# Routing attention and an MLP mixer: queries of the first pairs by rows of 1536 bytes, ahead of the keys, and an earlier turn of the second pair's queries

## Chip, cores and metric

The kernel runs on one core of a Trainium2 chip. The metric is the device time of one execution in microseconds (us): the median of three runs, and beside it one execution taken with the hardware profiler, from which all rows of the profile come. The core's engines are PE (TensorE, matmuls; PEld are its weight loads), DVE (VectorE), ACT (ScalarE), POOL (GpSimd) and SP (SyncE, which issues most transfers). Sixteen DMA engines carry the transfers.

## What is computed

Attention with a cluster mask for 4 batches of 8 heads, 768 tokens and 64 dimensions, then a mixer over tokens and over channels:

```python
q_assign = argmax(einsum('bhsd,hcd->bhsc', q_n, c_n), -1)   # c_n: 16 normed centroids a head
k_assign = argmax(einsum('bhsd,hcd->bhsc', k_n, c_n), -1)
mask = q_assign[:, :, :, None] == k_assign[:, :, None, :]
scores = where(mask, q @ k.T / 8, -1e9)
x = softmax(scores) @ v                                      # to (4, 768, 512)
u = x + (relu(x.T @ w_tok1) @ w_tok2).T                      # tokens: 768 -> 256 -> 768
out = u + relu(u @ w_ch1) @ w_ch2                            # channels: 512 -> 1536 -> 512
```

All is float32, and q, k, v, the centroids and the weights lie in HBM. The centroids must be normed; queries and keys need not be for the argmax.

## The kernel before

One tile, `arena`, holds everything in SBUF; `Buf` gives a view of it by offset. One PSUM tile `ps` has 8 banks. So the profile names nearly all operands `arena` and `ps`, and operations are told apart by line and shape.

**Order.** Nothing is issued directly. Every operation is recorded in a `Program` with the engines it may run on and a cost, what it reads and what it writes (`g.add`; `mm`, `turn`, `copy`, `tt`, `vec` and `dma` are wrappers, lines 844 to 906). `Program.run` plans: PE keeps the order of the recording; the other engines take, among the operations that are ready by the planned times, the one with the earliest due time. The plan gives one fixed order for each engine's queue and decides which of two allowed engines takes an operation. On the chip each queue runs in that order, and semaphores, which are set for overlapping ranges of a tile, hold an instruction back until its inputs are there. A change in a cost, in a transfer's planned time (`more`, `early`, `after`) or in the recording can therefore move instructions elsewhere.

**Stages.** 32 heads are worked in 16 pairs `m` of two heads. For a pair, keys and queries are laid as T: [128 = 2 heads x 64, 12 blocks of 128 tokens], six blocks of keys, then six of queries. `route(m)` multiplies T by the block matrix `cbd` of normed centroids (four matmuls of 32 columns, line 846), and DVE finds each token's cluster (lines 1098 to 1103: transpose from PSUM, maximum by group, comparison, transpose back). The result becomes, in bf16, a matrix M of 0 and a large number, which adds the mask to the scores as a second matmul. `scores(m)` does 12 chunks: first the plain scores (`plain`), then the mask matmul, then an exponential on ACT (line 1205). `values` multiplies by v (line 1238). Then come the token mixer (from about 325 us) and the channel mixer, both with seven products in place of eight, whose sums run on DVE and POOL.

**The start.** For pairs 3 and up, T is made with transfers (`part_qk`, `join_qk`). For the first three it is made on PE: `load_qk` brings keys and queries of a pair with four transfers of 192 KB, one for each head of each, to `qks`: 128 partitions, 6 tokens a partition, the two heads side by side, so in pieces of 256 bytes. `turn_qk` turns 12 blocks of [128 tokens, 2 x 64] with PE into three banks, and three copies of 128 x 512 bring them to T. `begin` (line 946) issues in this order: centroids on SP; k and q of pair 0, one head of each on SP and one on ACT; k and q of pair 1. While transfers run, `keep_busy(12)` multiplies the identity by itself on PE. `norm` (lines 980 to 998) is one operation on DVE, with a square root on ACT in its middle (line 984): it norms the centroids as soon as they have landed. They are turned on PE into bank 7 and copied to `cbd` with two DVE copies (line 867). `route(0, 3)` follows. Its masks go to `M0` in eight small placements (lines 1124 to 1136), each of which ACT or DVE may do. In `scores(0)` the first three chunks of plain scores and then the turns of pair 1 stand ahead of the first mask matmul; `route(1)` follows the third:

```python
        ahead = 3 if m == 0 else 0
        for n in range(ahead):
            plain(n)
        if m == 0:
            turn_qk(1, (7, 6, 7))
            load_qkr(3, 18.0)
```

Pair 2 is turned amid `values` of pair 0.

Of the kernel before, what the change touches and what calls it, by code (L numbers as in the profile page):

```python
# [15 lines left out]
ACT = mybir.ActivationFunctionType  # L16
# [31 lines left out]
W = 64  # L48
SUM_LO, SUM_HI = 1e-15, 1e15
GRAIN = 32  # L50
BUSY, HITS_AT = 12, 18.0
CHECK_AT = 532.0
FOLD = "-VVVVVVVVVV-----"

# [669 lines left out]
def kernel(  # L724
# [43 lines left out]
    def buf(kb, shape, dt=F32):  # L768
        return Buf(arena, int(kb * 256), shape, dt)
# [13 lines left out]
    rcps = [Buf(arena, 384 + 32 * i, [2, 2, NJ]) for i in range(2)]  # L783
    dall = Buf(arena, 448, [NP, 2, NJ])

    qks = [buf(3 + 6 * i, [2, NJ, 2, D]) for i in range(2)]
    vs = [buf(15 + 3 * i, [2, NJ, D]) for i in range(3)]
    Ts = [buf(24 + 6 * i, [NQK, P]) for i in range(3)]
    Ms = [buf(42 + 3 * i, [2, S], BF16) for i in range(2)]
# [50 lines left out]
    def bank(*i):  # L840
        return [("ps", n) for n in i]
# [56 lines left out]
    def vec(fn, c, rd, wr, early=0.0, after=0.0):  # L898
        return g.add({"DVE": c - 0.08}, lambda e: fn(), rd, wr, after=after, early=early)

    def dma(dst, src, rd, wr, kb, row, after=0.0, queue="SP"):

        q = {"SP": nc.sync, "ACT": nc.scalar, "POOL": nc.gpsimd}[queue]
        return g.add(
            {queue: ISSUE}, lambda e: q.dma_start(dst, src), rd, wr, (kb * 1024, row), after  # L905
        )

    def transpose(dst, src, rd, wr, kb):
# [3 lines left out]
        )  # L912


    def load_qk(m, after=0.0, queues=("SP", "SP")):
        b, hp = divmod(m, H // 2)
        t = qks[m % 2]
        for i, a in ((1, k), (0, q)):
            for h, qu in enumerate(queues):
                dma(  # L920
                    t.ap[:, i, :, h],
                    a[b, 2 * hp + h].rearrange("(p j) d -> p j d", p=P),
                    [], [("qk", m % 2, i, h)] + (t.rows(i, i + 1) if h else []), 192, 256,
                    after, qu,
                )

    def load_qkr(m, after=0.0):
        b, hp = divmod(m, H // 2)
# [16 lines left out]

    def begin():
        cen, sq = rt[0], rt[1]
        dma(cen.ap[:, 0:D], centroids.rearrange("h c d -> (h c) d"), [], cen.k(), 32, 256)
        load_qk(0, 0.0, ("SP", "ACT"))
        load_qk(1, 1.0)  # L950
        load_v(0, 9.0)
        load_v(1, 26.0)
        g.add({"POOL": 1.0}, lambda e: make_identity(nc, ident.ap), [], ident.k())
        def consts():
            nc.vector.memset(ones.ap, 1.0)
            nc.vector.memset(msc.ap[0 : P // 2, 0:1], 1.0)
# [12 lines left out]

        vec(consts, 0.8, [], ones.k() + msc.k() + cbd.k() + want.k() + unsc.k() + low.k())  # L970
        vec(lambda: nc.vector.memset(M0.ap, 0.0), 0.5, [], M0.k())
        keep_busy(BUSY)

        def col(i):
            return nsq.ap[:, i : i + 1]

        def norm(e):
            c = cen.ap[:, 0:D]
            ss, lo, nrm, rr, tw = (col(i) for i in range(5))
            nc.vector.tensor_tensor(out=sq.ap[:, 0:D], in0=c, in1=c, op=ALU.mult)  # L980
            nc.vector.reduce_sum(out=ss, in_=sq.ap[:, 0:D], axis=AX.X)

            nc.vector.tensor_scalar_max(out=lo, in0=ss, scalar1=float(2.0**-100))
            nc.scalar.sqrt(nrm, lo)

            for it in range(2):
                nc.vector.reciprocal(out=rr, in_=nrm)
                nc.vector.scalar_tensor_tensor(
                    out=tw, in0=ss, scalar=rr, in1=nrm, op0=ALU.mult, op1=ALU.add
                )  # L990
                nc.vector.tensor_scalar(
                    out=nrm, in0=tw, scalar1=0.5, scalar2=(1e-6 if it else 0.0),
                    op0=ALU.mult, op1=ALU.add,
                )
            nc.vector.reciprocal(out=rr, in_=nrm)
            for i in range(2):
                nc.vector.tensor_scalar_mul(
                    out=sq.ap[:, i * D : (i + 1) * D], in0=c, scalar1=rr
                )

        g.add({"DVE": 4.0}, norm, cen.k(), sq.k() + nsq.k())
        turn_qk(0, (0, 1, 2), (0, 1))
        turn(ps[:, 7, 0:P], sq.ap[:, 0:P], sq.k(), bank(7))
        turn_qk(0, (0, 1, 2), (2,))
        g.add(
            {"ACT": 1.5},
            lambda e: nc.scalar.activation(out=col(5), in_=col(1), func=ACT.Exp, scale=0.0),
            nsq.k() + Ts[0].k(), [("table",)],
        )
        for i in range(2):  # L1010
            copy(
                cbd.ap[i * D : (i + 1) * D, :, i * C : (i + 1) * C],
                ps[i * D : (i + 1) * D, 7, 0:P].rearrange("p (a i c) -> p a i c", i=2, c=C)[:, :, i],
                64, bank(7), cbd.k(), ("DVE",),
            )


        def own():
            nc.vector.tensor_reduce(
                out=heads.ap, in_=ident.ap.rearrange("p (a h c) -> p h a c", h=2, c=C),  # L1020
                axis=AX.XY, op=ALU.add,
            )
            for i in range(2):
                nc.vector.tensor_scalar(
                    out=msc0.ap[:, i], in0=heads.ap, scalar1=(BIG, -BIG)[i], scalar2=None,
                    op0=ALU.mult,
                )

        vec(own, 0.7, ident.k() + nsq.k(), heads.k() + msc0.k())

    def keep_busy(n):

        for _ in range(n):
            mm(ps[:, 5, 0:P], ident.ap, ident.ap, True, True, 0.22, ident.k(), bank(5))

    def turn_qk(m, banks, parts=range(3)):
        src, T = qks[m % 2], Ts[m % 3]
        for n in parts:
            bk = banks[n]
            for i in range(4):  # L1040
                a, j = divmod(4 * n + i, NJ)
                a = 1 - a
                turn(
                    ps[:, bk, i * P : (i + 1) * P],
                    src.ap[:, a, j].rearrange("p h d -> p (h d)"),
                    [("qk", m % 2, a, 0), ("qk", m % 2, a, 1)] + src.rows(a, a + 1), bank(bk),
                )

            copy(
                T.ap[:, 4 * n : 4 * n + 4].rearrange("p a t -> p (a t)"), ps[:, bk], 512,  # L1050
                bank(bk), T.rows(4 * n, 4 * n + 4),
            )

    def part_qk(m):
# [24 lines left out]
    def route(m, bk):  # L1079
# [4 lines left out]
        for gr in range(4):  # L1084
            r0 = (NJ + HJ * gr) % NQK
            mm(
                ps[32 * gr : 32 * gr + 32, bk, 0:HS], cbd.ap[:, hp],
                T.ap[:, r0 : r0 + HJ].rearrange("p a t -> p (a t)"), True, True, 0.161,
                T.rows(r0, r0 + HJ) + cbd.k(), bank(bk), pos=(0, 32 * gr),
            )  # L1090
        a, e, o = rt[0:3]
        if m == 0:
# [68 lines left out]
    def scores(m):  # L1161
# [8 lines left out]
        def plain(n):  # L1170
            u, i = chunk(n)
            s, r0 = n % 3, NJ + HJ * u
            for h in range(2):
                hs = slice(64 * h, 64 * h + 64)
                mm(
                    ps[:, 2 * s + h, 0:HS], T.ap[hs, i],
                    T.ap[hs, r0 : r0 + HJ].rearrange("p a t -> p (a t)"), True, False, 0.3225,
                    T.rows(i, i + 1) + T.rows(r0, r0 + HJ), bank(2 * s + h), pos=(64 * h, 0),
                )

        ahead = 3 if m == 0 else 0
        for n in range(ahead):
            plain(n)
        if m == 0:
            turn_qk(1, (7, 6, 7))
            load_qkr(3, 18.0)
        for n in range(2 * NJ):
            u, i = chunk(n)
# [139 lines left out]
    def pair(m):  # L1328
# [4 lines left out]
            next_qk(m)  # L1333
        for i in range(NJ):
            if i == 3 and m == 0:
                turn_qk(2, (1, 2, 3))
            if i == 4 and 1 <= m < NP - 2:
                route(m + 2, 0)
            if i == 1:
                if m:  # L1340
                    sums(m - 1, 5)
                    finish_x(m - 1, 5, 1)
                add_up(m)
            values(m, i)
# [624 lines left out]

    begin()  # L1970
    load_qk(2, 9.0)
    route(0, 3)
    token_weights()
    channel_weights(1, 12.0)
    channel_weights(2, 180.0)
# [80 lines left out]
```

## Time and profile before

| | us |
|---|---|
| median of three runs | 789.86 (789.45 to 791.11) |
| the profiled execution | 789.87 |
| its span, first to last instruction | 788.0 |
| PE busy | 777.8 |
| DVE busy | 675.2 |
| ACT busy | 461.4 |
| POOL busy | 194.1 |

Rows of the profile give times from the start of the span. A group row reads: line, engine, operation, out<-in by tile names, shapes, count | busy us, mean ns of one | idle time just before and what ended it. A row of a stretch of time gives the busy time of each engine in it, then the granted clock of PE (1.00 is full), the DMA engines' mean busy share and GB/s. Matmuls overlap in the pipeline, so a busy PE is not PE at its peak.

### The profile page before, as it was taken

Reading aid. Unit: us, or ns where it says so; the run is one execution under the profiler, and the core shown is the slowest. Engines: PE = TensorE matmul, PEld = TensorE weight load, DVE = VectorE, ACT = ScalarE, POOL = GpSimd, SP = SyncE. Lnnn points to the kernel's source line nnn. Section 1 sums busy time; section 2 is a strip of 40 time slices with the busy share of each in tenths; the row PEclk is TensorE's granted clock in tenths of the full one; section 3 lists DMA queues with packets and bytes.
Section 4 is the critical chain, followed back from the end, with each engine's and each line's share of the span. In section 5 each row is a group of like instructions: output and inputs, shape, how many; then the busy total and the mean of one; then the engine's idle time right before and its main releaser. Section 6 shows DMA issues by size and latency. Waiting matters only on the chain.

```text
span 788.0 us, 15324 instructions
## 1 busy us (share of the span) xinstructions
PE 777.8 (99%) x5975; PEld 463.1 (59%) x5975; DVE 675.2 (86%) x848; ACT 461.4 (59%) x614; POOL 194.1 (25%) x187
## 2 busy tenths in 40 slices
PE   8999999999999999999999999999999999999996
PEld 5666666666666666545555555555555555555554
DVE  6979999999998999999999877999853576799964
ACT  5788888889889875599614368633235204400422
POOL 0000000000000000001274598700285289830000
PEclk9999999999999999999999999999999999999999
DMA  9676668876778953568848999975788744444666
GB/s 249 169 192 180 170 154 221 212 202 178 196 196 215 266 178 128 127 135 202 195 124 253 313 281 266 273 189 132 168 189 177 165 100 101 105 105 102 160 164 161
DMA packets 326576, 143.68 MB, mean 182 GB/s; under 512 B 260192, under 2 KB 322400, under 8 KB 326496
## 3 DMA queue, kind: packets, MB, share of 16 engines
q1 hardware_dynamic: 324128, 141.83, 71.6%
q8 instruction: 49, 0.80, 0.4%
q10 hardware_dynamic: 2368, 0.79, 0.4%
q14 instruction: 31, 0.25, 0.1%
HBM read 91.95 MB, written 28.61 MB: 153 GB/s over the span
## 4 chain that ended last, share of the span: by engine, by line
PE 95%; DVE 3%; DMA 1%; issue 0%; ACT 0%; SPq 0%
PE ps L846 77%; PE ps L1238 18%; DVE arena L885 2%; DMA arena<-in_q_dram 1%; DMA arena<-in_moe_w_ch_dram 0%; ACT arena L865 0%; DVE arena L1384 0%; DVE arena L1390 0%; DVE arena L1387 0%; SPq L905 0%; DVE arena L1380 0%; DVE arena L867 0%; ACT arena L1129 0%
## 5 line engine op out<-in xcount | busy, mean ns | idle before, releaser
L846 PE MATMUL ps<-arena 128*128 128x384 f32 (+5 forms) x2727 | 640.2, 463 | 4.5 <-POOL arena masks.py:199 1.4
L846 PEld LDWEIGHTS ps<-arena 128*128 128x128 f32 (+2 forms) x2343 | 340.1, 184 | 250.3 <-issue 61.6
L885 DVE TENSOR_TENSOR arena<-arena 128x1536 f32<-128x1536 f32 (+6 forms) x340 | 369.9, 1109 | 12.5 <-issue 3.6
L885 POOL TENSOR_TENSOR arena<-arena 128x384 f32<-128x384 f32 x181 | 193.4, 1109 | 501.8 <-DVE arena L885 378.6
L885 DVE TENSOR_TENSOR arena<-ps,arena 128x384 f32<-128x384 f32 (+3 forms) x227 | 189.4, 844 | 78.4 <-PE ps L846 76.0
L875 ACT COPY arena<-arena 128x768 uint16<-128x768 uint16 x221 | 189.2, 955 | 62.6 <-DMA arena<-arena 32.8
L1205 ACT ACTIVATE arena<-ps 128x768 f32<-128x768 f32 x192 | 150.7, 811 | 35.2 <-PE ps L846 33.4
L1238 PE MATMUL ps<-arena 128*32 128x192 f32 (+1 forms) x3248 | 144.9, 335 | 0.0
L1238 PEld LDWEIGHTS ps<-arena 128*32 128x32 f32 x3248 | 103.7, 110 | 44.1 <-issue 15.6
L865 ACT COPY arena<-ps 128x512 f32<-128x512 f32 (+2 forms) x44 | 31.3, 719 | 116.1 <-PE ps L846 114.8
L892 ACT ACTIVATE arena<-arena 128x1152 f32<-128x1152 f32 (+1 forms) x38 | 39.7, 1070 | 51.0 <-DVE arena L885 50.3
L1912 ACT ACTIVATE arena<-arena 128x768 f32<-128x768 f32 x40 | 38.7, 969 | 32.8 <-DMA arena<-in_moe_w_ch_dram 27.1
L846 PEld LDWEIGHTS <-arena 64*128 64x128 bf16 x384 | 19.2, 94 | 24.6 <-issue 0.2
L1390 DVE SCALAR_TENSOR_TENSOR arena<-arena 128x512 f32<-128x512 uint32 (+1 forms) x31 | 21.5, 713 | 0.4
L1384 DVE SCALAR_TENSOR_TENSOR arena<-arena 128x512 uint32<-128x512 uint32 (+1 forms) x31 | 20.9, 695 | 0.3
L1108 ACT ACTIVATE arena<-arena 128x384 bf16<-128x384 f32 x16 | 11.2, 701 | 13.6 <-issue 13.6
L1380 DVE TENSOR_SCALAR arena<-arena 128x512 uint32<-128x512 uint32 (+1 forms) x31 | 13.9, 458 | 4.0 <-DMA arena<-in_moe_w_tok_dram 4.0
L1285 DVE STREAM_TRANSPOSE arena<-ps 128x768 f32<-128x768 f32 x16 | 15.2, 952 | 0.4 <-PE ps L1238 0.4
L1387 DVE TENSOR_SCALAR arena<-arena 128x512 uint32<-128x512 uint32 (+1 forms) x31 | 12.8, 436 | 0.4
L1293 DVE STREAM_TRANSPOSE arena<-ps 128x384 f32<-128x384 f32 x16 | 9.3, 579 | 2.2 <-PE ps L1238 2.0
L1098 DVE STREAM_TRANSPOSE arena<-ps 128x384 f32<-128x384 f32 x16 | 9.1, 571 | 1.8 <-PE ps L846 1.8
L1103 DVE STREAM_TRANSPOSE arena<-arena 128x384 f32<-128x384 f32 x16 | 9.3, 578 | 0.6
(57 smaller groups left out, 47.2 us busy)
## 6 DMA issues: line engine op xcount, KB each, us to landing
arena<-wd SPq DMA_DIRECT2D x196, 192.0 KB, 3.0
wd<-arena SPq DMA_DIRECT2D x84, 224.0 KB, 3.0
arena<-in_moe_w_ch_dram SPq DMA_DIRECT2D x96, 128.0 KB, 3.1
arena<-in_moe_w_ch_dram SPq DMA_DIRECT2D x16, 768.0 KB, 5.3
arena<-in_v_dram SPq DMA_DIRECT2D x16, 384.0 KB, 4.8
out_dram<-arena SPq DMA_DIRECT2D x14, 384.0 KB, 3.5
arena<-in_k_dram SPq DMA_DIRECT2D x13, 384.0 KB, 4.2
arena<-in_q_dram SPq DMA_DIRECT2D x13, 384.0 KB, 4.2
```

Source lines behind the costliest of these rows:

```text
L846: nc.tensor.matmul(dst, lhsT=lhsT, rhs=rhs, start=start, stop=stop, tile_position=pos, is_transpose=tr, skip_group_check=True,)
L865: nc.scalar.copy(out=dst, in_=src)
L875: nc.scalar.copy(out=dst, in_=src)
L885: (nc.vector if e == "DVE" else nc.gpsimd).tensor_tensor(out=dst, in0=a, in1=b, op=op)
L892: nc.scalar.activation(out=dst, in_=src, func=ACT.Relu)
L1205: lambda e, ex=ex, s=s, u=u: nc.scalar.activation(out=ex.ap[:, :, u * HS : (u + 1) * HS], in_=ps[:, 2 * s : 2 * s + 2, 0:HS], func=ACT.Exp ...
L1238: nc.tensor.matmul(dst, lhsT=lhsT, rhs=rhs, start=start, stop=stop, tile_position=pos, skip_group_check=True,)
L1285: lambda: nc.vector.transpose(out=x.ap[:, :, cols].rearrange("p j (c d) -> p c j d", d=32), in_=ps[:, 6:8, 0:HS],),
L1380: vec(lambda: nc.vector.tensor_scalar(out=hh, in0=hi, scalar1=0x07FFFFFF, scalar2=3, op0=ALU.bitwise_and, op1=ALU.logical_shift_left,), f, ...
L1384: vec(lambda: nc.vector.scalar_tensor_tensor(out=TT, in0=hi, scalar=0xC0000000, in1=hh, op0=ALU.bitwise_and, op1=ALU.bitwise_or), 0.14 + 0 ...
L1390: vec(lambda: nc.vector.scalar_tensor_tensor(out=ll, in0=lo, scalar=float(2.0**-52), in1=hh.bitcast(F32), op0=ALU.mult, op1=ALU.mult,), 0. ...
L1912: lambda e, i=i, func=func, bias=bias, n=n, hi=hi: nc.scalar.activation(out=hi, in_=hi, func=func, bias=bias, accum_out=wsum.ap[:, i, n : ...
```

## The change

- `qks` is split into `q0s` (for each head six tokens side by side) and `k0s` (the two heads side by side, as before).
- `load_qk` brings both heads' queries with one transfer of 384 KB in rows of 1536 bytes, ahead of the keys, and the keys as before in two of 192 KB in pieces of 256 bytes. For pair 0, the queries go on ACT's queue and the keys on SP's.
- `turn_qk` becomes `turn_q` and `turn_k`. `turn_q` turns, for each head, three blocks of two tokens x 64; one token of a block comes out in the upper and one in the lower half of the partitions, so two copies of 64 x 384 for each head bring them to every other block of T. `turn_k` turns two times three blocks and copies 128 x 384 twice.
- In `begin` the queries of pair 1 are turned right after the centroids, before `route(0)`, which moves to bank 6; the keys of pair 1 are turned after the first of the three chunks of plain scores.
- `keep_busy` does 7 matmuls instead of 12. Planned costs and times change: `more` of the centroids' transfer (-5.1) and of q and k (-0.7), the identity on POOL, `norm`, `own` (`early`).

```diff
-BUSY, HITS_AT = 12, 18.0
+BUSY, HITS_AT = 7, 18.0
...
-    qks = [buf(3 + 6 * i, [2, NJ, 2, D]) for i in range(2)]
+    q0s = [buf(3 + 6 * i, [2, NJ, D]) for i in range(2)]
+    k0s = [buf(6 + 6 * i, [NJ, 2, D]) for i in range(2)]
...
-    def load_qk(m, after=0.0, queues=("SP", "SP")):
+    def load_qk(m, after=0.0, queue="SP"):
         b, hp = divmod(m, H // 2)
...
+        tq, tk = q0s[m % 2], k0s[m % 2]
+        dma(
+            tq.ap.rearrange("p h j d -> p h (j d)"),
+            q[b, 2 * hp : 2 * hp + 2].rearrange("h (p j) d -> p h (j d)", p=P),
+            [], tq.k(), 384, 1536, after, queue, -0.7,
+        )
+        for h in range(2):
+            dma(
+                tk.ap[:, :, h], k[b, 2 * hp + h].rearrange("(p j) d -> p j d", p=P),
+                [], [("k0", m % 2, h)] + (tk.k() if h else []), 192, 256, after, more=-0.7,
+            )
...
-        dma(cen.ap[:, 0:D], centroids.rearrange("h c d -> (h c) d"), [], cen.k(), 32, 256)
-        load_qk(0, 0.0, ("SP", "ACT"))
+        dma(
+            cen.ap[:, 0:D], centroids.rearrange("h c d -> (h c) d"), [], cen.k(), 32, 256,
+            more=-5.1,
+        )
+        load_qk(0, 0.0, "ACT")
         load_qk(1, 1.0)
...
-        g.add({"POOL": 1.0}, lambda e: make_identity(nc, ident.ap), [], ident.k())
+        g.add({"POOL": 0.2}, lambda e: make_identity(nc, ident.ap), [], ident.k())
...
-        g.add({"DVE": 4.0}, norm, cen.k(), sq.k() + nsq.k())
-        turn_qk(0, (0, 1, 2), (0, 1))
-        turn(ps[:, 7, 0:P], sq.ap[:, 0:P], sq.k(), bank(7))
-        turn_qk(0, (0, 1, 2), (2,))
+        g.add({"DVE": 3.0}, norm, cen.k(), sq.k() + nsq.k())
+        turn_q(0, (0, 1))
+        turn_k(0, (2, 3))
+        turn(ps[:, 6, 0:P], sq.ap[:, 0:P], sq.k(), bank(6))
+        turn_q(1, (4, 7))
...
-        vec(own, 0.7, ident.k() + nsq.k(), heads.k() + msc0.k())
+        vec(own, 0.7, ident.k(), heads.k() + msc0.k(), early=9.0)
...
+    def turn_q(m, banks):
+
+        src, T = q0s[m % 2], Ts[m % 3]
+        for h, bk in enumerate(banks):
+            for i in range(HJ):
                 turn(
                     ps[:, bk, i * P : (i + 1) * P],
+                    src.ap[:, h, 2 * i : 2 * i + 2].rearrange("p j d -> p (j d)"),
+                    src.k(), bank(bk),
                 )
+            for j in range(2):
+                copy(
+                    T.ap[D * h : D * h + D, NJ + j : NQK : 2],
+                    ps[D * j : D * j + D, bk, 0:HS].rearrange("p (i t) -> p i t", t=P), HS,
+                    bank(bk),
+                    [("tq", m, j)] if h
+                    else sum((T.rows(NJ + i, NJ + i + 1) for i in range(j, NJ, 2)), []),
+                )
...
         for n in range(ahead):
+            if n == 1:
+                turn_k(1, (7, 6))
             plain(n)
         if m == 0:
-            turn_qk(1, (7, 6, 7))
             load_qkr(3, 18.0)
...
-                turn_qk(2, (1, 2, 3))
+                turn_q(2, (1, 2)), turn_k(2, (3, 4))
...
-    route(0, 3)
+    route(0, 6)
```

`turn_k` is `turn_qk` for the keys alone, with blocks of three; matmuls that read T's queries also wait for the keys `("tq", m, j)`.

More of the change, by code (lines that the diff above doesn't have):

```diff
@@ L899, in vec, with dma @@
         return g.add({"DVE": c - 0.08}, lambda e: fn(), rd, wr, after=after, early=early)
-    def dma(dst, src, rd, wr, kb, row, after=0.0, queue="SP"):
+    def dma(dst, src, rd, wr, kb, row, after=0.0, queue="SP", more=0.0):
         q = {"SP": nc.sync, "ACT": nc.scalar, "POOL": nc.gpsimd}[queue]
         return g.add(
-            {queue: ISSUE}, lambda e: q.dma_start(dst, src), rd, wr, (kb * 1024, row), after
+            {queue: ISSUE}, lambda e: q.dma_start(dst, src), rd, wr, (kb * 1024, row), after,
+            more=more,
         )
@@ L912, in transpose @@
         )
-    def load_qk(m, after=0.0, queues=("SP", "SP")):
+    def load_qk(m, after=0.0, queue="SP"):
         b, hp = divmod(m, H // 2)
[L917 to L925, printed above, removed]
+        tq, tk = q0s[m % 2], k0s[m % 2]
[9 more added lines that the diff above has]
+            )
     def load_qkr(m, after=0.0):
@@ L1012, in begin @@
                 cbd.ap[i * D : (i + 1) * D, :, i * C : (i + 1) * C],
-                ps[i * D : (i + 1) * D, 7, 0:P].rearrange("p (a i c) -> p a i c", i=2, c=C)[:, :, i],
-                64, bank(7), cbd.k(), ("DVE",),
+                ps[i * D : (i + 1) * D, 6, 0:P].rearrange("p (a i c) -> p a i c", i=2, c=C)[:, :, i],
+                64, bank(6), cbd.k(), ("DVE",),
             )
@@ L1027, in own, with turn_k @@
                 )
-        vec(own, 0.7, ident.k() + nsq.k(), heads.k() + msc0.k())
+        vec(own, 0.7, ident.k(), heads.k() + msc0.k(), early=9.0)
     def keep_busy(n):
         for _ in range(n):
[L1034 to L1042, printed above, removed]
+            mm(ps[:, 5, 0:P], ident.ap, ident.ap, True, True, 0.43, ident.k(), bank(5))
+    def turn_q(m, banks):
+        src, T = q0s[m % 2], Ts[m % 3]
+        for h, bk in enumerate(banks):
+            for i in range(HJ):
                 turn(
                     ps[:, bk, i * P : (i + 1) * P],
-                    src.ap[:, a, j].rearrange("p h d -> p (h d)"),
-                    [("qk", m % 2, a, 0), ("qk", m % 2, a, 1)] + src.rows(a, a + 1), bank(bk),
+                    src.ap[:, h, 2 * i : 2 * i + 2].rearrange("p j d -> p (j d)"),
[8 more added lines that the diff above has]
+                    else sum((T.rows(NJ + i, NJ + i + 1) for i in range(j, NJ, 2)), []),
+                )
+    def turn_k(m, banks):
+        src, T = k0s[m % 2], Ts[m % 3]
+        for n, bk in enumerate(banks):
+            for i in range(HJ):
+                turn(
+                    ps[:, bk, i * P : (i + 1) * P],
+                    src.ap[:, HJ * n + i].rearrange("p h d -> p (h d)"),
+                    [("k0", m % 2, 0), ("k0", m % 2, 1)] + src.k(), bank(bk),
                 )
             copy(
-                T.ap[:, 4 * n : 4 * n + 4].rearrange("p a t -> p (a t)"), ps[:, bk], 512,
-                bank(bk), T.rows(4 * n, 4 * n + 4),
+                T.ap[:, HJ * n : HJ * (n + 1)].rearrange("p a t -> p (a t)"), ps[:, bk, 0:HS], HS,
+                bank(bk), T.rows(HJ * n, HJ * (n + 1)),
             )
@@ L1088, in route @@
                 T.ap[:, r0 : r0 + HJ].rearrange("p a t -> p (a t)"), True, True, 0.161,
-                T.rows(r0, r0 + HJ) + cbd.k(), bank(bk), pos=(0, 32 * gr),
+                T.rows(r0, r0 + HJ) + cbd.k() + [("tq", m, j) for j in range(2)], bank(bk),
+                pos=(0, 32 * gr),
             )
@@ L1177, in plain @@
                     T.ap[hs, r0 : r0 + HJ].rearrange("p a t -> p (a t)"), True, False, 0.3225,
-                    T.rows(i, i + 1) + T.rows(r0, r0 + HJ), bank(2 * s + h), pos=(64 * h, 0),
+                    T.rows(i, i + 1) + T.rows(r0, r0 + HJ) + [("tq", m, j) for j in range(2)],
+                    bank(2 * s + h), pos=(64 * h, 0),
                 )
```

## The prediction

> **What bounds the kernel now.** I read the busy time by stage first, then PE's waits, then the chain of waits from the start of the span, because the change touches only the first microseconds. Busy time in four stretches (start:end, length, then busy time of each engine, granted clock, DMA share, GB/s):
>
> ```profile
> 0.00:8.89 8.89, 6.16 (x37) 5.71 (x37) 4.33 (x32) 3.23 (x6) 0.70 (x6) 1.00 0.92 171
> 14.63:381.00 366.37, 366.32 (x4658) 220.70 (x4658) 345.15 (x463) 303.15 (x402) 5.90 (x6) 1.00 0.72 186
> 381.00:411.00 30.00, 29.00 (x87) 15.84 (x86) 29.20 (x48) 10.01 (x11) 17.02 (x16) 1.00 0.68 170
> 411.00:781.00 370.00, 370.00 (x1153) 217.21 (x1152) 290.43 (x295) 141.52 (x191) 170.48 (x160) 1.00 0.73 180
> ```
>
> From 14.63 on PE has work without a gap, but for 1.00 us in 381 to 411. A microsecond won or lost before 14.63 is therefore won or lost at the end. PE's waits (waiter <- releaser: us, times, longest):
>
> ```profile
> PE ps L846 <- POOL arena masks.py:199: 1.4, 1, 1.4
> PE ps L846 <- DVE arena L885: 1.3, 4, 0.5
> PE ps L846 <- ACT arena L865: 0.9, 2, 0.7
> PE ps L846 <- DMA arena<-in_q_dram: 0.7, 1, 0.7
> ```
>
> All but the second row lie in the start. The chain of waits there (start, us, what):
>
> ```profile
> 1.93 5.20 DMA arena<-in_q_dram
> ...
> 7.26 0.42 PE ps L846 x2
> ...
> 7.71 1.14 ACT arena L865 x2
> ...
> 8.89 3.71 PE ps L846 x24
> ...
> 14.63 1.38 PE ps L846 x10
> ```
>
> The last half of the first pair's queries lands at 7.13, is turned on PE, copied by ACT, and at 8.89 the first routing matmuls (`route(0)`) start. Those rows decide the masks, and once three chunks are masked `route(1)` starts at 14.63. Routing also needs the centroids, but they are early: they are the first transfer on SP's queue. The timeline (start, us, what):
>
> ```profile
> 0.74 0.40 SPq L905 DMA_DIRECT2D arena<-in_centroids_dram  x1
> 1.19 0.69 SPq L905 DMA_DIRECT2D arena<-in_k_dram  x1
> 2.60 0.23 DVE L980 TENSOR_TENSOR arena<-arena 128x64 f32<-128x64 f32 x1 [0.28 <-DMA arena<-in_centroids_dram]
> 3.41 0.20 ACT L984 ACTIVATE arena<-arena 128x1 f32<-128x1 f32 x1
> 5.12 0.42 DVE L997 TENSOR_SCALAR arena<-arena 128x64 f32<-128x64 f32 x2
> 7.82 0.46 DVE L867 COPY arena<-ps 64x64 f32<-64x64 f32 x2 [1.81 <-PE ps L846]
> 9.81 0.58 DVE L1098 STREAM_TRANSPOSE arena<-ps 128x384 f32<-128x384 f32 x1 [1.54 <-PE ps L846]
> 11.61 0.58 DVE L1103 STREAM_TRANSPOSE arena<-arena 128x384 f32<-128x384 f32 x1
> 13.85 0.28 PEld L846 LDWEIGHTS <-arena 64*128 64x128 bf16 x6 [0.17 <-issue]
> 14.37 0.47 SPq L905 DMA_DIRECT2D arena<-in_q_dram  x1
> ```
>
> **What the change does to this chain.** In the built program SP issues k0 (two heads), q1, then the centroids; ACT's queue carries q0 alone. DVE's order is: `norm`, one of the four q0 copies, the two `cbd` copies, two q1 copies, then the routing chain. ACT's is: the square root of `norm`, two q0 copies, the third q0 copy, two k0 copies, two q1 copies. Three semaphore waits in it matter. ACT's third q0 copy waits for DVE's q0 copy, since their interleaved rows of T overlap as ranges; DVE's two q1 copies wait for ACT's for the same reason; and all of ACT's copies are queued behind the square root, which waits for the centroids. So nearly the whole start now hangs on the landing of the centroids. Call C the time at which DVE takes them (2.60 now).
>
> *From C to route(1).* Prices of the copies and placements, by shape (count | busy, mean ns | idle):
>
> ```profile
> L865 ACT COPY arena<-ps 128x384 f32<-128x384 f32 x15 | 7.2, 479 | 58.1 <-PE ps L846 56.9 <-DVE arena L885 1.2
> L867 DVE COPY arena<-ps 128x384 f32<-128x384 f32 x5 | 2.8, 550 | 0.2 <-PE ps L846 0.2
> ...
> L1131 DVE TENSOR_SCALAR arena<-arena 32x384 bf16<-32x384 f32 x4 | 1.9, 474 | 0.1
> L1136 DVE CAST arena<-arena 32x384 bf16<-32x384 f32 x3 | 1.1, 350 | 0.1
> L1129 ACT CAST arena<-arena 32x384 bf16<-32x384 f32 x1 | 0.5, 507 | 0.0
> ```
>
> No 64x384 copy is in the trace; I take the 128x384 one, since a copy's free size is the same (a quarter less or more on each of them moves the sum by 0.5). Step by step:
> - `norm` ends 5.54 - 2.60 = 2.94 after C. DVE's q0 copy (0.55) ends at C+3.5, the `cbd` copies (0.46) at C+3.97. The turn of the centroids hides under the first.
> - ACT's third q0 copy starts at C+3.5 and takes 0.48; the two k0 copies end at C+4.95, and the last of the four `route(0)` matmuls needs the last of them: C+5.0. ACT's q1 copies end at C+5.9.
> - From the start of `route(0)` to DVE's reading it is 9.81 - 8.89 = 0.92: C+5.9. But DVE must first do its two q1 copies behind ACT's: about C+5.45 to 6.0 and 6.0 to 6.55. So the routing chain starts at C+6.55, and lasts 12.19 - 9.81 = 2.38 as now: C+8.95.
> - Placements: DVE 0.47 + 0.35, ACT one activation (0.51 if it costs what the cast does) and a cast 0.51, now in parallel: ACT ends at C+10.0, where now it took DVE and ACT until 13.85, 1.66 after the chain. That is the one gain, some 0.6.
> - Three chunks of masks to `route(1)`: now 14.63 - 13.85 = 0.78, of which some waits for a copy of T1. With 0.7, `route(1)` starts at **C+10.75**. PE's other work (first scores, turns of pair 1) fits inside.
>
> Now it starts at 14.63, so the change gains if C is below 14.63 - 10.75 = **3.9** and loses otherwise.
>
> *C itself.* Landings and rates (issue to landing in us, then four stretches with GB/s last; 6.00:8.50 moves 256-byte rows, 10.00:11.00 mostly rows of 1536):
>
> ```profile
> arena<-in_k_dram SPq DMA_DIRECT2D x1, 192.0 KB, 4.2
> ...
> arena<-in_centroids_dram SPq DMA_DIRECT2D x1, 32.0 KB, 1.8
> ```
>
> ```profile
> 6.00:8.50 2.50, 1.52 (x13) 1.07 (x10) 0.45 (x3) 1.38 (x3) 0.00 (x0) 1.00 1.32 214
> 10.00:11.00 1.00, 1.00 (x8) 0.76 (x6) 0.95 (x2) 0.35 (x2) 0.00 (x0) 1.00 1.05 376
> 1.30:4.70 3.40, 3.34 (x15) 3.34 (x16) 2.38 (x10) 1.49 (x2) 0.01 (x1) 1.00 0.76 173
> 4.70:5.70 1.00, 1.00 (x11) 1.00 (x10) 0.90 (x6) 0.00 (x0) 0.00 (x0) 1.00 1.33 239
> ```
>
> Now the centroids land at 2.57, the next transfer on SP's queue at 1.19 + 4.2 = 5.4, the one behind it at 7.13: in order of issue. After the change three issues stand ahead of theirs: 0.74 + 0.69 + 0.69 + 0.47 and gaps of 0.04, so they are issued near 2.7 and land at 4.5 even with nothing queued. Queued are q0 and q1 (393 KB each, 1.05 at 376) and k0 (393 KB, 1.84 at 214, 1.64 at 239), with 0.15 of their own: 3.9 to 4.1. On a start of 2.4 (the present landing less its own transfer) C is 6.3 to 6.5. From the other side: 7.13 less the 819 KB that preceded it (3.83 at 214) gives a start of 3.3 and C = 7.4. I take **6.8**, a little nearer to the first, since rows of 1536 bytes fill the queue faster from the start. The rows of 1536 are a real gain of 1.6 for q0 and q1 together, but they are spent ahead of the wrong wait.
>
> `route(1)` then starts at 6.8 + 10.75 = 17.55, 2.9 later than now.
>
> *The rest.* Five `keep_busy` matmuls go (24 passes of 0.21 and less before, 14 now, until about 4.35); they were hidden by the wait for q at 7.13, so this alone is nothing. Pair 2's turns make six copies instead of three: ACT 4 x 0.48 for 3 x 0.57, DVE 2 x 0.55 more, around 30 to 40. They hide under PE's matmuls, as DVE has 366.37 - 345.15 = 21 us idle in that stretch; uncovered they would cost 1.1. SP issues fewer transfers for q; nobody waits for that. PE's order from the fourth chunk on is unchanged, and POOL's throughout.
>
> **Sum.** The profiled execution took 789.87 (span 788.0 and 1.87 around it), equal to the median 789.86. 789.87 + 2.9 = **792.8**. C from 6.3 to 7.4 and 0.3 for the copies give 792.0 to 793.7 for this case.
>
> **Rivals.**
> 1. *The centroids are not held by the queue* (the side that is not slower). They land 1.8 after their issue, C = 4.55, `route(1)` at 15.3: +0.7, **790.5**. Below C = 3.9 it would be a gain, but three issues ahead of theirs exclude that unless they shrink by 0.7. The Trainium skill (DMA: Bandwidth & Descriptors, "Queues, rings and completion order") says that completion is not first-in-first-out per issuing engine, a later transfer may finish its write earlier; by that rule a small one could slip past. Against it stand the three landings above, in order and 1.8 to 2.8 apart.
> 2. *PE's clock falls back.* In the two last rows above, matmul passes of the same kind follow every 3.40/16 = 0.21 us until 4.7 and every 0.10 after it: PE runs at half pace in its first 3.4 us. After the change PE is busy only until about 4.35 and a few turns, then has little until C+5 = 11.8. If it is slow again then, the two chunks of scores ahead of the masks (some 1.3 of the 3.71 in the row at 8.89) take twice as long and pass C+10 by 0.6, and masks and `route(1)` lose another 0.9: +1.5 (0.9 to 2.5 as the slowness ends sooner or later), **794.3**. The rows show clock 1.00 throughout, and PE's waits in the start are at most 1.4; no gap this long is in the trace. The Trainium skill (TensorE: Matmul & The Clock Gate, Part 1) has the clock halved by default and after an idle window of about 3.4 us, free-running; the first 3.4 us agree with it, and by that rule the gap here is just long enough.
> 3. *381 to 411 gives some back.* PE waits there for DVE 1.3 us in all; if DVE's chain there does not shift with PE, up to 1.3 of the loss is absorbed: **791.5**. Against it: DVE starts each of its pieces from PE's results.
>
> **Chances.** The forecast case 0.55, rival 1 0.13, rival 2 0.20, rival 3 0.08; 0.04 is left for centroids as early as now (C = 2.6: 1.3 gained) together with the 1.3 of 381 to 411, 787.3. Range 790.3 to 795.2: it takes in rival 1's price and most of rival 2's. Anything within 0.2% (1.6 us) counts as no change, about what a measurement of this kernel can tell. Rival 1 and a third or so of rival 3, whose price lies on that line, fall there: 0.16. The rest of the four is slower, 0.80, and the last case faster, 0.04.
>
> **What would show it.** Right: DVE's first `norm` instruction starting at 6 to 7.4 after a wait for `in_centroids`, ACT's square root as late, `route(1)` at 17 to 18, and from there the same length as now. Wrong: centroids landing before 5, ACT's q0 copies before 5, or the first mask matmul near 14 or earlier; a half-pace PE after 10 would be rival 2; an end that moves less than `route(1)` does, rival 3.

## The result, and the profile after

| | before | after |
|---|---|---|
| median, us | 789.65 (789.19 to 791.11, 6 runs) | 793.82 (793.08 to 794.26, 6 runs) |
| the profiled execution / its span | 789.87 / 788.0 | 793.80 / 791.9 |
| DVE takes the centroids (C) | 2.60 | 7.90 |
| `route(1)` starts | 14.63 | 18.55 |

The ratio is 1.005, with a 95% interval of 1.0037 to 1.0063: slower by about 4.2 us. The forecast was 792.8, in a range of 790.3 to 795.2; it gave slower a chance of 0.80.

PE's longest waits in the whole span of the kernel after (waiter <- releaser: us, times, longest):

```profile
PE ps L847 <- DVE arena L1004: 3.4, 1, 3.4
PE ps L847 <- POOL arena masks.py:199: 1.4, 1, 1.4
PE ps L847 <- DMA arena<-in_k_dram: 1.3, 1, 1.3
PE ps L847 <- DVE arena L886: 1.3, 4, 0.5
```

The first row is new. Line 1004 is the last step of `norm`: PE waits 3.4 us for normed centroids. The third is new too: PE waits 1.3 for the last keys of pair 0, where before it waited 0.7 for queries. The last row, the waits of 381 to 411, is as before. The chain of waits from the start (start, us, what):

```profile
2.85 5.02 DMA arena<-in_centroids_dram
...
10.31 0.43 DVE arena L1004 x2
...
10.79 5.00 PE ps L847 x22
...
16.70 0.70 ACT arena L1149
...
17.98 8.89 PE ps L847 x67
```

The chain now begins with the centroids. Before, it began with pair 0's queries. The timeline shows how the copies queue up behind them (start, us, what, [idle before <- releaser]):

```profile
2.17 0.64 SPq L906 DMA_DIRECT2D arena<-in_q_dram  x1
2.85 0.47 SPq L906 DMA_DIRECT2D arena<-in_centroids_dram  x1
7.90 0.22 DVE L987 TENSOR_TENSOR arena<-arena 128x64 f32<-128x64 f32 x1 [5.17 <-DMA arena<-in_centroids_dram]
8.60 0.20 ACT L991 ACTIVATE arena<-arena 128x1 f32<-128x1 f32 x1 [6.13 <-DVE arena L990]
11.35 2.21 ACT L866 COPY arena<-ps 64x384 f32<-64x384 f32 x5 [1.70 <-DVE arena L868]
13.10 1.15 DVE L868 COPY arena<-ps 64x384 f32<-64x384 f32 x2 [1.30 <-ACT arena L866]
14.28 0.58 DVE L1122 STREAM_TRANSPOSE arena<-ps 128x384 f32<-128x384 f32 x1
...
18.55 0.16 PEld L847 LDWEIGHTS ps<-arena 128*32 128x32 f32 x8 [0.32 <-issue]
```

ACT sits behind its square root until 8.60, then waits 1.70 for DVE's copy; DVE then waits 1.30 for ACT's. The routing chain starts at 14.28, where before it started at 9.81, and the last row is the start of `route(1)`. Busy time by stretch (start:end, length, busy time of PE, PEld, DVE, ACT and POOL, granted clock, DMA share, GB/s):

```profile
0.00:18.55 18.55, 12.46 (x65) 8.09 (x65) 9.97 (x43) 8.64 (x17) 0.70 (x6) 0.91 0.85 240
18.55:381.00 362.45, 362.40 (x4647) 218.61 (x4647) 341.79 (x458) 300.18 (x399) 3.92 (x4) 1.00 0.71 183
381.00:415.00 34.00, 33.02 (x99) 18.11 (x98) 32.94 (x56) 13.92 (x15) 19.26 (x18) 1.00 0.69 168
```

From `route(1)` on PE is full again and loses the same 1.0 us beyond 381. From the first matmul of `route(1)` to PE's last, the kernel before takes 782.31 - 14.63 = 767.68 and the kernel after 786.13 - 18.55 = 767.58. So the whole loss, 3.92 of 3.9 us in the span, stands ahead of `route(1)`. A narrower stretch of the start:

```profile
12.00:14.00 2.00, 2.00 (x9) 0.55 (x8) 0.87 (x2) 1.96 (x5) 0.00 (x0) 0.50 1.18 309
```

PE is granted half its clock here, after the gap of 3.36 us that ends at 10.79; before, no stretch of the start was below 1.00.

### The profile page after: what moved, and what is told of

It reads as the page before. It is cut to its first block, busy times and chain, and to the rows that moved or that the text cites. A ratio compares the mean times of both kernels' runs of the same rounds, so it can differ in the third digit from the quotient of the medians.

```text
span 791.9 us, 15301 instructions
## 1 busy us (share of the span) xinstructions
PE 778.7 (98%) x5965; PEld 462.3 (58%) x5965; DVE 675.9 (85%) x851; ACT 464.2 (59%) x620; POOL 193.5 (24%) x187
## 4 chain that ended last, share of the span: by engine, by line
PE 94%; DVE 3%; DMA 1%; issue 0%; SPq 0%; ACT 0%
PE ps L847 76%; PE ps L1264 18%; DVE arena L886 2%; DMA arena<-in_centroids_dram 1%; DMA arena<-in_moe_w_ch_dram 0%; DVE arena L1410 0%; DVE arena L1416 0%; SPq L906 0%; DVE arena L1413 0%; DVE arena L1406 0%; ACT arena L1149 0%; DVE arena L868 0%; ACT arena L1153 0%; ACT arena L866 0%; DVE arena L995 0%
## 5 line engine op out<-in xcount | busy, mean ns | idle before, releaser
L866 ACT COPY arena<-ps 128x384 f32<-128x384 f32 (+3 forms) x48 | 32.2, 677 | 116.5 <-PE ps L847 114.5
L1132 ACT ACTIVATE arena<-arena 128x384 bf16<-128x384 f32 x16 | 11.2, 702 | 15.1 <-issue 15.1
L868 DVE COPY arena<-ps 128x384 f32<-128x384 f32 (+3 forms) x14 | 8.7, 621 | 3.0 <-ACT arena L866 1.5
L1319 DVE STREAM_TRANSPOSE arena<-ps 128x384 f32<-128x384 f32 x16 | 9.2, 577 | 1.3 <-PE ps L1264 1.2
```

Source lines behind the costliest of these rows:

```text
L866: nc.scalar.copy(out=dst, in_=src)
```

## The experiments

The theory under test: the centroids' place in SP's queue sets C, and C sets everything to `route(1)`. The rivals: the waits between ACT and DVE, the earlier turn of pair 1's queries, PE's clock.

**Centroids first.** After the planning, one step of the order is moved; nothing else changes on any engine.

```diff
-        for o, e in best[1]:
+        order = best[1]
+        i = [o for o, e in order].index(self.moved)   # the centroids' transfer
+        step = order.pop(i)
+        sp = [i for i, (o, e) in enumerate(order) if e == "SP"]
+        order.insert(sp[0], step)
+        for o, e in order:
             o.fn(e)
```

> The kernel after with one thing moved: SP issues the centroids first instead of fourth; the order of every other engine is as in the kernel after. Theory (the place of the centroids in the queue is what the change costs): DVE takes them at about 2.6 instead of 7.90, norm ends near 5.5, and the start is then held by what is late next, the keys of pair 0 (about 6.5) and the queries of pair 1 (about 7.7), whose turns stand ahead of route(0) on PE. DVE's last q1 copies end near 10.1 instead of 14.25, route(1) starts near 14.4 instead of 18.55, and the time is 789.6 (788.8 to 790.4), about the kernel before. Rival (waits between ACT and DVE on interleaved rows of T, or more copies, hold the start): route(1) stays at 17 or later, 792 or more. Rival (the loss lies behind the start): 793.8 whatever route(1) does.

Measured: 789.34 (789.14 to 790.75, 12 runs) against 789.58 before, ratio 0.9992 (0.9975 to 1.0009). Its timeline, then its chain of waits:

```profile
3.17 0.23 DVE L992 TENSOR_TENSOR arena<-arena 128x64 f32<-128x64 f32 x1 [0.44 <-DMA arena<-in_centroids_dram]
```

```profile
2.61 5.18 DMA arena<-in_q_dram
...
9.51 0.56 DVE arena L873
...
13.80 8.89 PE ps L852 x67
```

C is 3.17, a little later than the 2.6 I expected, and DVE's last copy ends at 10.07, as expected; masks come 4.2 us earlier than after. The place of one transfer in a queue makes the whole difference. All that the change does besides gains nothing that can be told: pair 1's queries, landing at 7.79, now begin the chain, because their turns stand ahead of `route(0)`.

**Centroids third.** The same move, to `sp[2]`: only the queries of pair 1 and the centroids change places.

> The kernel after with one exchange in SP's order: the centroids third, behind the keys of pair 0 and ahead of the queries of pair 1, instead of fourth; every other engine's order is unchanged. Theory (each transfer ahead of the centroids costs the time that it takes on the DMA engines): they land about 0.3 behind the last keys of pair 0 (6.44), C = 6.8 instead of 7.90, everything to route(1) moves by 1.1, time 792.7 (792.2 to 793.3). Rival (the small transfer is held by whatever else is in flight, in any place but the first): C of 7.5 or more, 793.4 or more.

Measured: 792.32 (791.72 to 793.30, 5 runs), ratio 1.0037 (1.0023 to 1.0051). The chain:

```profile
2.17 3.90 DMA arena<-in_centroids_dram
...
16.17 8.89 PE ps L852 x67
```

C is 6.09 instead of the 6.8 expected. DVE's whole program up to 123 us shifts by -1.81 against the kernel after, and the masks by 17.98 - 16.17 = 1.81. So one transfer of 393 KB ahead of the centroids costs them 1.81 us. That would be 217 GB/s if nothing else moved meanwhile, but it is no rate of this transfer alone: the keys issued before it are late as well, since their second half lands at 5.84 here and at 6.44 to 6.76 in the six profiled runs with the order of the kernel after.

**The kernel before with its centroids fourth.** The same move in the kernel before, to `sp[3]`.

> The kernel before with one thing moved: SP issues the centroids fourth, behind one head of keys and one of queries of pair 0 and one head of keys of pair 1, instead of first; the order of every other engine is as in the kernel before. Theory: DVE takes them at about 8.0 instead of 2.60; norm ends near 10.9, the last third of pair 0's turns stands behind the turn of the centroids on PE, and route(0) starts near 12.1 instead of 8.89: 789.65 + 3.2 = 792.9 (792.2 to 793.8), that is, most of the loss of the change without any other part of it. Rival (small transfers pass the queue: C near 4.5): below 790.5. Rival (the loss comes from the turns and copies of the change): 789.7.

Measured: 795.60 (794.05 to 803.80, 12 runs), ratio 1.0066 (1.0047 to 1.0086). The profiled execution is the 803.8, with a second dip of PE's clock far behind the start, so only its start is read:

```profile
12.00:14.00 2.00, 1.32 (x9) 0.20 (x8) 0.00 (x0) 1.79 (x2) 0.00 (x0) 0.50 1.04 194
14.00:16.00 2.00, 2.00 (x10) 1.14 (x8) 1.53 (x3) 0.28 (x2) 0.00 (x0) 0.50 0.90 213
16.00:18.00 2.00, 2.00 (x9) 0.77 (x7) 1.86 (x5) 0.00 (x0) 0.00 (x0) 0.64 0.50 203
```

C was 7.94, as expected, but the time was not: `route(0)` came at 12.83, the first mask matmul at 19.88 and `route(1)` at 20.65, 6.0 later than before, with PE at half pace from 11 to 17. So the late transfer of 32 KB, with the half pace that follows it, costs the old kernel 6.0; the whole change costs 4.2, and the two intervals overlap. To separate the clock, the next run keeps PE busy in that gap.

**The same, with PE busy.** 12 matmuls of the identity are issued ahead of the turn of the centroids (`g.busy` is the body of `keep_busy`, outside the plan).

```diff
         for o, e in order:
+            if o is self.late:                        # the turn of the centroids
+                for _ in range(12):
+                    self.busy("PE")
             o.fn(e)
```

> The kernel before with the centroids issued fourth, as in the experiment that gave 795.6, and 12 matmuls of the identity (2.7 us) on PE ahead of the turn of the centroids, to fill PE's gap of 2.86 there. Theory (that experiment lost 3.2 by the late centroids, as expected, and the rest by PE at half pace from 10.8 to 17): granted clock 1.00 from 8 on, route(0) near 12.0 instead of 12.83, the first mask matmul near 17.0 instead of 19.88, time 789.6 + 3.1 = 792.7 (792.2 to 793.5). Rival (the clock is not what made it 795.6): 795 or more.

Measured: 794.89 (794.25 to 796.05, 5 runs), ratio 1.0068 (1.0054 to 1.0081). A stretch of its start, and its chain:

```profile
12.00:14.00 2.00, 1.71 (x14) 0.82 (x16) 0.76 (x2) 1.72 (x3) 0.00 (x0) 1.00 1.30 234
```

```profile
3.12 4.82 DMA arena<-in_centroids_dram
...
12.29 3.72 PE ps L854 x24
...
18.02 8.32 PE ps L854 x62
```

The start behaved nearly as expected: clock 1.00, `route(0)` at 12.29, the first mask matmul at 17.26 instead of 19.88, `route(1)` 3.39 later than before. The time did not: that accounts for 793.0. In the profiled execution another 1.1 comes at 499.5 us, where DVE waits 1.05 for POOL, which the kernel before does not do there, and 1.4 behind PE's last matmul (793.95 - 786.83 = 7.12 to the end of the span, 5.70 before). I did not find what sets these off, and the other runs, 794.25 to 796.05, are about as long. So the 3.4 of the late centroids are shown, and about 2 us of this variant stay open.

**Queries' copies on ACT alone.**

```diff
                     else sum((T.rows(NJ + i, NJ + i + 1) for i in range(j, NJ, 2)), []),
+                    ("ACT",) if m < 2 else ("ACT", "DVE"),
```

> The kernel after with the four copies of queries of pairs 0 and 1 each allowed on ACT alone, so that none of them waits for a copy of the other engine; the planner then gives one keys' copy to DVE and shares the placements otherwise. The centroids stay fourth. Theory: C stays at 7.9, and only the waits across the engines go, worth 0.5 to 1.1 us: route(1) near 17.7, 792.9 (792.4 to 793.8). Rival (those waits are the main part of the loss): below 791.

Measured: 793.90 (792.98 to 795.52, 12 runs), ratio 1.0048 (1.0031 to 1.0065): no gain. From the timeline:

```profile
14.05 0.58 DVE L1123 STREAM_TRANSPOSE arena<-ps 128x384 f32<-128x384 f32 x1 [2.32 <-PE ps L847]
```

DVE no longer waits for ACT, but 2.3 us for PE, which is at half pace (granted clock 0.50 in 12 to 16). One wait took the other's place, and the chain starts only 0.23 earlier. The edit is not a pure one either: the planner now puts a copy of pair 1's keys on DVE behind the chain (0.56 us), so the placements start at 17.05 instead of 16.69.

**PE kept busy in the kernel after.** Three sizes, each ahead of the turn of the centroids; first 26 and 14 matmuls, recorded at a planned cost of 0:

```diff
+        keep_busy(26, 0.0)      # second run: keep_busy(14, 0.0)
         turn(ps[:, 6, 0:P], sq.ap[:, 0:P], sq.k(), bank(6))
```

> The kernel after with 26 more matmuls of the identity by itself on PE ahead of the turn of the centroids, in the 3.4 us in which PE waits for them; all other orders are unchanged. It tells what the half pace of PE in 11 to 14.5 costs. Theory (it is hidden: DVE reads the result of route(0) only after its own q1 copies, which end at 14.25, and the three chunks of scores are done before the masks): turns and routing matmuls run at full pace, time unchanged, 793.8 (793.3 to 794.3). Rival (the clock is a part of the loss): 793.2 or less.

> The kernel after with 14 matmuls of the identity by itself on PE ahead of the turn of the centroids; all other orders are unchanged. In the run with 26 they took 0.22 us each (two passes of 0.111) and so 5.8 us, more than the gap of 3.36 that they were to fill, and route(0) came 2.2 us late; 14 take 3.1. Theory (the half pace of PE from 11 to 14.5 is hidden behind the copies): granted clock 1.00 from 8 on instead of 0.50 in 12 to 14, DVE's last q1 copies still end near 14.2, time 793.8 (793.2 to 794.2). Rival (the clock is a part of the loss): 793.1 or less.

Measured: 794.62 (793.98 to 796.72, 12 runs; ratio 1.0059, 1.0042 to 1.0076), above the expected range, and 793.56 (793.33 to 794.03, 5 runs; ratio 1.0050, 1.0037 to 1.0064), within it. Both sets of matmuls outlasted the gap. With 26, DVE's last q1 copy (of pair 1's queries) ended at 15.68 instead of 14.25; with 14 at 14.72, since PE was itself at half pace, 0.213 us a pass, from 6.9 until 10.5, and each matmul is two passes. Then 7, issued outside the plan as in the run of the kernel before, with the copies as they are and with the copies on ACT alone:

> The kernel after with 7 matmuls of the identity on PE ahead of the turn of the centroids (with 14 PE was still at half pace, 0.213 a pass, when they began, and they delayed the turn by 1.7 us); the other engines' orders are unchanged. Theory (in the kernel after the half pace of PE is hidden by DVE's copies behind ACT's): granted clock 1.00 throughout, routing chain still at 14.2 to 14.3, time 793.7 (793.3 to 794.1). Rival (the clock costs by itself): 793.1 or less.

> The kernel with the queries' copies on ACT alone (793.9), with 7 matmuls of the identity on PE ahead of the turn of the centroids; the other engines' orders are as there. Theory (the waits across the engines and PE's half pace hide each other: in that run DVE no longer waited for ACT, but 2.32 us for PE, whose granted clock was 0.50 from 12 to 16): with both gone the routing chain starts near 13.0 instead of 14.05, the first mask matmul comes near 17.3 instead of 18.34, and the time is 792.8 (792.3 to 793.4). Rival (the waits or the clock cost nothing at all, only the centroids do): 793.9.

Measured: 793.32 (793.20 to 793.89, 5 runs; ratio 1.0045, 1.0031 to 1.0059) with the copies as they are, 792.54 (792.38 to 794.04, 5 runs; ratio 1.0035, 1.0021 to 1.0049) with the copies on ACT. From the first of them, stretch and timeline:

```profile
12.00:14.00 2.00, 2.00 (x12) 0.66 (x12) 0.87 (x2) 1.96 (x5) 0.00 (x0) 1.00 1.16 298
```

```profile
13.10 1.15 DVE L870 COPY arena<-ps 64x384 f32<-64x384 f32 x2 [1.30 <-ACT arena L868]
14.28 0.58 DVE L1124 STREAM_TRANSPOSE arena<-ps 128x384 f32<-128x384 f32 x1
17.59 2.65 PE L849 MATMUL ps<-arena 64*128 64x384 bf16 x18 [0.64 <-DVE arena L1162]
```

At full clock the routing chain starts at the same 14.28, the first mask matmul at the same 17.59 and `route(1)` at the same 18.55: PE now waits 0.64 for the placements instead of being late. The half pace is hidden in the kernel after; the median is 0.5 lower, but the intervals overlap. With both removed the median is 793.82 - 792.54 = 1.3 lower, as expected, but here too the intervals overlap. The profiled execution of that run was its slowest (794.04). In it the routing chain starts at 13.12, against 14.05 and 14.28 with one of the two removed. But PE, after a wait of 1.76, again falls to half pace, and `route(1)` starts only 0.08 before the 18.55 of the kernel after (a stretch, then a row of the timeline):

```profile
14.00:16.00 2.00, 2.00 (x9) 1.15 (x7) 1.86 (x4) 1.14 (x2) 0.00 (x0) 0.53 0.78 288
```

```profile
18.47 0.16 PEld L849 LDWEIGHTS ps<-arena 128*32 128x32 f32 x8 [0.32 <-issue]
```

The other four took 792.38 to 792.63. That they kept full pace would explain the 1.3, but no trace shows it.

**Towards a better version.** With the centroids first, pair 1's queries hold the start, so I turned them later, without and with PE kept busy:

```diff
-        turn_q(1, (4, 7))                  # ahead of route(0)
...
             if n == 1:
+                turn_q(1, (4, 7))
+            if n == 2:
                 turn_k(1, (7, 6))
             plain(n)
```

> The kernel after with the centroids issued first on SP, and the turns of pair 1's queries moved from ahead of route(0) to after the first chunk of plain scores (its keys' turns to after the second). Theory (with the centroids first, what holds the start is the landing of pair 1's queries at 7.8, whose turns and copies stand ahead of the routing chain): route(0) starts near 8.1 instead of 8.64 and the routing chain near 9.0 instead of 10.11; one of DVE's q1 copies now stands inside the chain (0.56), so the first mask matmul comes near 12.9 instead of 13.42: 788.8 (788.2 to 789.4). Rival (something else holds the start there, the keys' landing or the placements): 789.3 or more.

> The kernel of the experiment in which pair 1's queries are turned later (791.25), with 8 matmuls of the identity added on PE, six ahead of the turns of pair 0's keys and two ahead of route(0); the other engines' orders are as there. In that run PE's granted clock was 0.62 in 8 to 12, its turns of pair 1's queries took 1.2 us instead of 0.66 and one of DVE's q1 copies, which stands inside the routing chain, waited for them, so that the chain took 4.5 us instead of 2.38. Theory (where PE's pace is not hidden behind copies, its gap is what costs): granted clock 1.00 from 8 on, the first mask matmul near 14 instead of 15.70, time 789.5 (788.8 to 790.3). Rival (the order alone costs it, the clock does nothing): 791 or more.

Measured: 791.25 (789.23 to 792.29, 10 runs; ratio 1.0008, 0.9986 to 1.0029) and 789.96 (789.42 to 790.63, 12 runs; ratio 0.9999, 0.9983 to 1.0015). The same stretch of the one and of the other:

```profile
8.00:12.00 4.00, 3.36 (x15) 1.08 (x15) 2.14 (x5) 2.04 (x4) 0.00 (x0) 0.62 1.10 340
```

```profile
8.00:12.00 4.00, 3.81 (x33) 2.31 (x31) 1.86 (x5) 2.58 (x5) 0.00 (x0) 1.00 1.08 336
```

Here the clock is on the path: DVE's q1 copy inside the routing chain waits for turns at half pace. With 8 more matmuls of the identity the first mask matmul comes at 14.94 instead of 15.70 and `route(1)` at 15.83 instead of 16.59, a gain of 0.76 in the traces; 14 was expected for the first of them. The medians differ by 1.3, but their intervals overlap. The order itself gains nothing over the kernel with the centroids first. A last version, with the centroids first:

```diff
+                    ("ACT",) if m == 1 else ("ACT", "DVE"),       # pair 1's queries' copies
...
         g.add({"DVE": 3.0}, norm, cen.k(), sq.k() + nsq.k())
+        g.add({"ACT": 1.5}, ...)          # loads the table of the exponential; stood after turn_q(1)
```

> The kernel after with the centroids issued first on SP, pair 1's queries' copies on ACT alone, and the dummy exponential that loads ACT's table recorded right after norm instead of after pair 1's turns. Theory (with the centroids first, what holds the routing chain is DVE's two q1 copies behind ACT's, until 10.07 against 9.5 for the result of route(0), and ACT's table load of 1.28 us stands between its copies): the chain starts near 9.5 instead of 10.11, the first mask matmul comes near 12.9 instead of 13.42: 788.8 (788.3 to 789.3). Rival (the keys' turns of pair 1 and the chunks ahead of the masks on PE take the place of that wait): 789.3.

Measured: 790.69 (789.40 to 798.18, 12 runs), ratio 1.0011 (0.9983 to 1.0039): missed. The chain:

```profile
8.26 0.57 DVE arena L873
...
8.88 1.44 PE ps L852 x8
...
10.34 0.59 DVE arena L1128
```

The planner gave DVE one of the keys' copies (8.26), so `route(0)` started at 8.88 and the routing chain at 10.34 instead of 9.5. No version beat the kernel before by more than can be measured; the one with the centroids first, 789.34, comes nearest.

## Why the prediction held, and which term was off

**The path from C.** Each step of the sum against the trace, as time after C:

| step | forecast | after |
|---|---|---|
| `norm` ends | 2.94 | 2.83 |
| `cbd` copies end | 3.97 | 3.90 |
| last matmul of `route(0)` can start | 5.0 | 4.85 |
| DVE's q1 copies end | 6.55 | 6.35 |
| routing chain ends | 8.95 | 8.76 |
| `route(1)` starts | 10.75 | 10.65 |

The price of the copies that the trace before did not show was good (last column: mean ns in the group rows, count | busy, mean ns | idle):

```profile
L866 ACT COPY arena<-ps 64x384 f32<-64x384 f32 x8 | 3.8, 471 | 4.3 <-PE ps L847 2.5 <-DVE arena L868 1.7
L868 DVE COPY arena<-ps 64x384 f32<-64x384 f32 x4 | 2.2, 557 | 1.6 <-ACT arena L866 1.5
```

They take 471 and 557 against the 479 and 550 of 128x384. With the centroids third (C 6.09) `route(1)` starts at 16.74, that is C + 10.65 again. With them first (C 3.17) it is 14.38, C + 11.2: pair 1's queries hold it there, which the sum did not have. In every profiled variant of the kernel after, the stretch from the first matmul of `route(1)` to PE's last one is 767.4 to 767.9, so the end moves with this start and with little else.

**C was mis-sized.** The sum counted what is issued up to the centroids, 1.21 MB, and put what is issued behind them at nothing. That step failed. In the kernel after, the stretch from the sum's start to the landing, and what the two queues had moved by the landing at 7.88 (queue q1 is SP's, q10 is ACT's; packets, MB, share of 16 engines):

```profile
2.40:7.88 5.48, 3.72 (x23) 3.27 (x22) 0.30 (x3) 0.07 (x1) 0.00 (x0) 1.00 1.09 272
```

```profile
q1 hardware_dynamic: 3451, 1.22, 65.7%
q10 hardware_dynamic: 272, 0.39, 15.7%
```

At 272 GB/s the 1.21 MB would take 4.5 us at most and give C = 6.9 or less, about the forecast. But SP's queue had moved 1.22 MB, and only 0.82 of these were issued up to the centroids: the other 0.40 MB, most of it the keys of pair 1, was issued behind them and moved first. With the centroids third it is the same, 0.76 MB on SP's queue by 6.07, of which 0.43 were issued up to them. Why the later packets get ahead is not shown. In the terms of the sum, the term that came out too small is "q0 and q1 (393 KB each, 1.05 at 376)": the place behind q1 cost 1.81, so 0.76 of the 1.10 by which C = 6.8 fell short of 7.90 is here; the other 0.34 is not traced to a term. The upper bound of 7.4 failed with it, since it left out the same bytes. All 1,212 KB at 214 GB/s would have given 2.4 + 5.7 = 8.1, close to 7.90 but by luck, as the engines moved 272 GB/s. The rest of the loss follows: 3.9 in the span instead of 2.9.

**Rival 1**, centroids not held by the queue, did not happen: 5.02 from issue to landing against 1.8. The rule of the Trainium skill behind it (DMA: Bandwidth & Descriptors, "Queues, rings and completion order", no first-in-first-out completion for an issuing engine) does not show in this start: SP's first landings, 5.09, 6.44, 7.59, 7.88, 8.53, 9.34, are in order of issue.

**Rival 2**, PE's clock, happened in its mechanism and not in its price. The clock fell to 0.50 after a gap of 3.36, and cost nothing measurable, because DVE's q1 copies behind ACT's ended later still. I had priced it at 1.5. Taken away alone, neither it nor those waits brings a gain that can be told. With both taken away the routing chain starts 1.16 earlier in the trace; the 1.3 of the medians is likely, but not shown.

**Rival 3**, 381 to 411 giving back up to 1.3, did not happen: 1.3 in 4 waits, as before.

**"`keep_busy` 12 to 7 is nothing"** held as far as the runs go, though none changes the count alone. The cover is not the wait for the queries that I named: in the kernel after PE waits 1.3 for the last keys and then 3.4 for the centroids.

## What to carry to other kernels

Issue a small transfer on which a whole stage waits first. Here 32 KB behind 1.2 MB came 5.3 us late, and moving that one issue to the front gave back all of the lost time. The bytes issued ahead of it are not the whole price: here another 0.4 MB issued behind it moved before it landed. A time that is planned for a transfer (here 5.1 us taken off) should be held against its landing. Where two waits end close together, removing one tells little about either (the chain started at 14.05 and 14.28); remove both (13.12).

## What was not expected of the hardware

PE fell to half pace after gaps much shorter than the 3.36 of the kernel after. Its granted clock was 0.53 after a longest wait of 1.76, and 0.62 in 8 to 12 in the run with the centroids third, whose longest wait was 2.1. It was 0.62 in 8 to 12 also in the run that turns pair 1's queries later, after a longest wait of only 1.3; in two other runs it stayed at 1.00 with waits of 1.4 and 1.5. The Trainium skill (TensorE: Matmul & The Clock Gate, Part 1) names an idle window of about 3.4 us, free-running; the fall after 3.36 is near that, those after 1.3, 1.76 and 2.1 with few matmuls around them do not follow from the gap's length alone. In the first 3 us passes are 0.213 apart too, yet the granted clock of the profile reads 1.00 there, and in the run with 14 matmuls it reads 1.00 while passes stay 0.213 apart until 10.5; a half pace of that kind is seen only in the spacing of the matmuls.
